# Attention and a Mish MLP on one core: the MLP in two phases through DRAM, with seven block products for w_out

## The chip, the cores and the metric

One core of one Trainium2 chip runs the whole program. The metric is device time in microseconds for one execution, from the first to the last instruction of the core. The engines are TensorE (PE, its weight loads PEld), VectorE (DVE), ScalarE (ACT), GpSimd (POOL) and SyncE (SP), which issues nearly all DMAs.

## The reference

Attention with a learned relative bias feeds a two-layer MLP with a Mish gate. All in float32; batch 4, 8 heads, 576 positions, 64 per head, so 2304 tokens of 512, and a hidden width of 2048.

```python
scores = scale * np.matmul(q, k.transpose(0, 1, 3, 2)) + bias        # bias: a small MLP of the relative position
attn = np.exp(scores - scores.max(-1, keepdims=True)); attn /= attn.sum(-1, keepdims=True) + 1e-09
x = np.matmul(attn, v).transpose(0, 2, 1, 3).reshape(2304, 512)
h = x @ w_in                                                          # 2304 x 2048
sp = np.where(h > 20.0, h, np.log1p(np.exp(np.minimum(h, 20.0))))
out = (h * np.tanh(sp)) @ w_out                                       # 2304 x 512
```

## The kernel before

The order of the work is written out by hand; each engine executes its instructions in program order and waits on semaphores.

**Bias stage** (to about 68 us). The relative bias of every head is computed and written to DRAM.

**Attention.** 16 pairs of heads and batches, each with five row groups c, make 80 steps; `step(n)` issues scores (PE, L220), the bias addition with the row maximum (DVE, L237), the exponentials (ACT, L252), the transposes of the step two before (PE, L287 and L290, evacuated by ACT, L295 and L296) and products with v (PE, L313, evacuated by DVE, L320). Two PSUM tiles hold the scores of one step. At the end of a step `split(n)` issues nine or ten pieces per five steps of the weights' conversion: w_in and w_out arrive as 64-bit floats and become 32-bit ones in four operations for a block of 128 x 512 (L118, or L116 on ACT; L121, L123, L125). All 32 blocks are converted here.

**MLP.** Every matmul is done three times with operands split in a high and a low part (`hi`, `lo`, float32r): hi x hi, hi x lo, lo x hi. Tokens go in blocks of 512, 512, 256, 512, 512. `hidden` (L589) makes 128 rows of h transposed for one block, 12 matmuls; `gate` computes the Mish as h * (e*e + 2e) / (e*e + 2e + 2) with e = exp(h), by ACT (Exp, Ln, Exp, a copy for ghi) and DVE (L595, L596, L606, L607, L612); `project` (L627) adds the product with 128 rows of w_out to the y tiles of the block in PSUM, three units behind `hidden`. The next block's x is loaded two units ahead of its splitting (`split_x`).

Of the kernel before, what the change touches and what calls it, by code (L numbers as in the profile page):

```python
# [16 lines left out]
HP = H // 2  # L17
# [9 lines left out]
E20 = 485165195.40979  # L27
# [4 lines left out]
NFC = DFF // P  # L32

# [11 lines left out]
def kernel(ctx: ExitStack, tc, qk, v, wb, w2, w_in, w_out, psia, psi4, rinv, eye, out):  # L45
# [21 lines left out]
    xa = sbuf("xa", side="right")  # L67
    dram = ctx.enter_context(tc.tile_pool(name="dram", bufs=1, space=DRAM))


    two = const.tile([P, 96], F32, name="two")
# [9 lines left out]
    order = [(kind, g, k) for g in range(4) for kind in "io" for k in range(4)]  # L81
    order.sort(key=lambda job: 4 * job[1] + (3.5 + job[2] if job[0] == "o" else 0))


    EARLY, MID = 4, 15
    MIDDLE = EARLY + MID
    ring = sbuf("ring").ring((len(order) - EARLY) * 2048 + 2560)
    w_hi, w_lo = {}, {}
    todo, w64, w32 = list(order), [], []

    def alloc_weights(jobs, p):
        for job in jobs:
            w_hi[job] = p.tile([P, 512], F32R, name="wh{}{}{}".format(*job))
            w_lo[job] = p.tile([P, 512], F32R, name="wl{}{}{}".format(*job))
# [12 lines left out]
    def conv_weights(on_act):  # L107

        job, w = w64.pop(0)
        late = order.index(job) >= EARLY
        c = (ring if late else convp).tile([P, 512], F32, name="w32")
        cu = c.bitcast(U32)
        if on_act:
            act.mul(c, w.bitcast(F32)[:, :, 1], 2.0 ** -112)  # L116
        else:
            dve.tensor_scalar(c, w.bitcast(F32)[:, :, 1], 2.0 ** -112, None, op0=ALU.mult)  # L118

        def parts():  # L120
            dve.tensor_scalar(w[:, :, 0], w[:, :, 0], 29, None, op0=ALU.logical_shift_right)  # L121
            yield False
            dve.scalar_tensor_tensor(cu, cu, 3, w[:, :, 0], op0=ALU.logical_shift_left, op1=ALU.bitwise_or)  # L123
            yield False
            dve.scalar_tensor_tensor(cu, w[:, :, 1], 0x80000000, cu, op0=ALU.bitwise_and, op1=ALU.bitwise_or)  # L125
            w32.append((job, c))
            yield True
        return parts()

    def split_weights(eng):  # L130
        job, c = w32.pop(0)
        if job not in w_hi:
            w_hi[job] = ring.tile([P, 512], F32R, name="wh{}{}{}".format(*job))
            w_lo[job] = ring.tile([P, 512], F32R, name="wl{}{}{}".format(*job))
        act.copy(w_hi[job], c)
        eng.tensor_tensor(w_lo[job], c, w_hi[job].bitcast(F32), op=ALU.subtract)
# [48 lines left out]
    def load_bias(hp, c):  # L185
# [3 lines left out]
        if c < 3 and hp % 2 == 0:  # L189
            pool_, name = ((xa, "xhi"), (xa, "xlo"), (x0, "xraw"))[c]  # L190
            t = pool_.tile([P, HP * TB], F32, name=name)[:, :2 * S]
        else:
            t = biasp.tile([P, 2 * S if c < 4 else S], F32, name=f"bias{c}")
# [135 lines left out]
    alloc_weights(order[:EARLY], wpool)  # L329

    x_raw, x_hi, x_lo = {}, {}, {}
    blocks = [(0, 512), (512, 512), (1024, 256), (1280, 512), (1792, 512)]

    def load_x(blk, p):
        t0, n = blocks[blk]
        raw = p.tile([P, HP, TB], F32, name="xraw", bufs=1)
# [19 lines left out]
    def ahead(n):  # L356
# [7 lines left out]
        if n == NS - 11:  # L364
            load_x(0, x0)
        if n == NS - 10:
            x_hi[0] = xa.tile([P, HP, TB], F32R, name="xhi")
            x_lo[0] = xa.tile([P, HP, TB], F32R, name="xlo")
# [8 lines left out]
    def split(n):  # L377

        i, x = divmod(n, 5)
        for _ in range(((2, 1, 2, 2, 2) if n > 25 else (2, 1, 3, 2, 2) if n > 4 else (0,) * 5)[x]):  # L380
            if not conv and w64:
                conv.append(conv_weights(x == 2))
            elif conv and next(conv[0]):
                conv.clear()
                load_weights()
                if w32[0][0] in order[:EARLY]:
                    split_weights(pool)
# [69 lines left out]
    dve.memset(two, 2.0)  # L457
# [99 lines left out]
    xp = sbuf("xp", 1, side="right")  # L557
    mp = sbuf("mp", 2, side="right")
    h_ps = psum("h_ps", 4, side="right")

    XPARTS = [(x, d) for x in "hl" for d in range(HP)]

    def split_x(blk, parts):
        n = blocks[blk][1]
        if blk not in x_hi:
            x_hi[blk] = (xp if blk % 2 else xa).tile([P, HP, TB], F32R, name="xhi")
# [8 lines left out]

    units = [(blk, tuple(range(f, f + TB // n))) for blk, (_, n) in enumerate(blocks) for f in range(0, NFC, TB // n)]
    h_t, gs, ys = {}, {}, {}

    LAG2 = 3

    def hidden(blk, fs):
        n = blocks[blk][1]
        h = h_ps.tile([P, TB], F32, name="h")
        for u, f in enumerate(fs):
            g4, r = divmod(f, 4)
            k = 0
            for w, x in ((w_hi, x_hi[blk]), (w_lo, x_hi[blk]), (w_hi, x_lo[blk])):
                for d in range(HP):
                    pe.matmul(h[:, u * n:(u + 1) * n], w["i", g4, d][:, r * P:(r + 1) * P], x[:, d, :n],  # L589
                              start=(k == 0), stop=(k == 11))  # L590
# [6 lines left out]
        h_t[blk, fs] = (h, e)  # L597

# [143 lines left out]
```

## Time and profile before

| | |
|---|---|
| median of 3 runs | 701.15 us (699.9, 701.15, 702.38) |
| span of the profiled execution | 700.9 us |
| PE, DVE, ACT, POOL busy | 672.9, 517.3, 458.4, 72.4 us |
| DMA | 81.88 MB, mean 117 GB/s |

Busy times are unions over the span. A PE instruction's end is modelled, so the time of a matmul in a stream is read from the distance of two starts. "Idle before" is what an engine waited ahead of an instruction, with the releaser behind the arrow.

### The profile page before, as it was taken

Reading aid. Unit: us, or ns where it says so; the run is one execution under the profiler, and the core shown is the slowest. Engines: PE = TensorE matmul, PEld = TensorE weight load, DVE = VectorE, ACT = ScalarE, POOL = GpSimd, SP = SyncE. Lnnn points to the kernel's source line nnn. Section 1 sums busy time; section 2 is a strip of 40 time slices with the busy share of each in tenths; the row PEclk is TensorE's granted clock in tenths of the full one; section 3 lists DMA queues with packets and bytes.
Section 4 is the critical chain, followed back from the end, with each engine's and each line's share of the span. In section 5 each row is a group of like instructions: output and inputs, shape, how many; then the busy total and the mean of one; then the engine's idle time right before and its main releaser. Section 6 shows DMA issues by size and latency. Waiting matters only on the chain.

```text
span 700.9 us, 13630 instructions
## 1 busy us (share of the span) xinstructions
PE 672.9 (96%) x5156; PEld 511.2 (73%) x5156; DVE 517.3 (74%) x1082; ACT 458.4 (65%) x987; POOL 72.4 (10%) x85
## 2 busy tenths in 40 slices
PE   5878999999999999999999999999999999999997
PEld 2224666776777666668888888889988888888886
DVE  7995898888988878868788566655775567665554
ACT  6895988888899888876675544444554455454443
POOL 0000142322222222710000000000000000000000
PEclk9999999999999999999999999999999999999999
DMA  4997688787778767204000120023005000010001
GB/s 150 318 285 228 195 273 263 216 284 225 245 234 266 241 231 240 55 22 116 1 1 0 66 56 1 1 76 106 1 1 150 1 1 0 1 60 1 1 0 60
DMA packets 46081, 81.88 MB, mean 117 GB/s; under 512 B 14400, under 2 KB 23104, under 8 KB 46016
## 3 DMA queue, kind: packets, MB, share of 16 engines
q1 hardware_dynamic: 43568, 72.70, 32.8%
q0 software_dynamic: 1872, 8.09, 3.9%
q8 instruction: 40, 0.66, 0.4%
q10 hardware_dynamic: 576, 0.22, 0.1%
q14 instruction: 25, 0.20, 0.1%
HBM read 60.60 MB, written 20.40 MB: 116 GB/s over the span
## 4 chain that ended last, share of the span: by engine, by line
PE 71%; ACT 9%; DVE 7%; DMA 3%; issue 2%; DVEq 0%; ACTq 0%
PE h L589 28%; PE y L627 28%; PE o L313 5%; PE s L220 5%; ACT pt L252 5%; DVE pt L237 4%; ACT main L295 3%; PE tp L287 3%; PE tp L290 1%; DMA w<-in_w_in_dram 1%; DMA w<-in_w_out_dram 1%; PE o L317 1%; DVE w L123 1%; DVE x L320 1%; DVE w L125 1%
## 5 line engine op out<-in xcount | busy, mean ns | idle before, releaser
L252 ACT ACTIVATE pt<-pt,m 128x576 f32<-128x576 f32 x144 | 112.2, 780 | 33.5 <-DVE m L237 32.9
L627 PE MATMUL y<-who,ghi 128*128 128x512 f32 x288 | 112.1, 389 | 0.0
L627 PE MATMUL y<-wlo,ghi 128*128 128x512 f32 x288 | 112.1, 389 | 0.0
L627 PE MATMUL y<-who,glo 128*128 128x512 f32 x288 | 112.0, 389 | 0.0
L611 ACT CAST ghi<-e 128x512 fp32r<-128x512 f32 x72 | 44.7, 621 | 93.5 <-DVE e L607 93.5
L237 DVE CUSTOM_DVE_ANT_0 pt<-s,bias 128x576 f32<-128x576 f32 (+1 forms) x112 | 81.3, 753 | 17.8 <-PE s L220 16.6
L594 ACT ACTIVATE e<-h 128x512 f32<-128x512 f32 x72 | 43.0, 597 | 65.9 <-PE h L589 65.7
L595 DVE TENSOR_SCALAR e<-e 128x512 f32<-128x512 f32 x72 | 30.6, 426 | 74.0 <-ACT e L594 74.0
L612 DVE TENSOR_TENSOR glo<-e,ghi 128x512 fp32r<-128x512 f32 x72 | 49.8, 692 | 44.9 <-ACT ghi L611 44.9
L589 PE MATMUL h<-xhi,whi 128*128 128x512 f32 (+1 forms) x320 | 79.1, 369 | 0.0
L589 PE MATMUL h<-xhi,wli 128*128 128x512 f32 (+1 forms) x320 | 78.7, 368 | 0.0
L589 PE MATMUL h<-xlo,whi 128*128 128x512 f32 (+1 forms) x320 | 78.7, 368 | 0.0
L313 PE MATMUL o<-main,vt 128*64 128x320 f32 (+1 forms) x512 | 73.8, 411 | 3.1 <-DVE x L320 3.0
L295 ACT COPY main<-tp 128x512 f32<-128x512 f32 x126 | 66.5, 577 | 2.0 <-DMA bias_d<-bt 1.9
L287 PE MATMUL tp<-ident,pt 64*128 64x64 f32 x1184 | 61.7, 227 | 6.3 <-ACT main L295 4.7
L589 PEld LDWEIGHTS h<-xhi,whi 128*128 128x128 f32 x320 | 57.1, 188 | 11.7 <-issue 0.7
L287 PEld LDWEIGHTS tp<-ident,pt 64*128 64x128 f32 x1184 | 53.5, 139 | 15.2 <-ACT main L295 13.1
L589 PEld LDWEIGHTS h<-xhi,wli 128*128 128x128 f32 x320 | 56.9, 189 | 10.0
L589 PEld LDWEIGHTS h<-xlo,whi 128*128 128x128 f32 x320 | 56.9, 189 | 10.0
L627 PEld LDWEIGHTS y<-who,glo 128*128 128x128 f32 x288 | 54.1, 188 | 11.3
L627 PEld LDWEIGHTS y<-who,ghi 128*128 128x128 f32 x288 | 54.1, 188 | 11.0
L627 PEld LDWEIGHTS y<-wlo,ghi 128*128 128x128 f32 x288 | 54.1, 188 | 10.9
(69 smaller groups left out, 1126.9 us busy)
## 6 DMA issues: line engine op xcount, KB each, us to landing
bias_d<-bt SPq DMA_DIRECT2D x36, 295.5 KB
w<-in_w_in_dram SPq DMA_DIRECT2D x16, 512.0 KB
w<-in_w_out_dram SPq DMA_DIRECT2D x16, 512.0 KB
qkhi<-in_qk_dram POOLq DMA_DIRECT2D x13, 608.0 KB, 4.5
rawqk<-in_qk_dram SPq DMA_DIRECT2D x13, 608.0 KB
vt<-in_v_dram SPq DMA_DIRECT2D x16, 320.0 KB
out_dram<-w SPq DMA_DIRECT2D x17, 256.0 KB
x_d<-x SPq DMA_DIRECT2D x32, 128.0 KB
```

What stands on the lines that cost most here:

```text
L220: pe.matmul(s[:, j, :SH], q[rows, c * P:(c + 1) * P], k[rows, KO + j * SH:KO + (j + 1) * SH], start=(t == 0), stop=(t == len(terms) - 1))
L237: dve.tensor_tensor_reduce(out=halves(pt[rows, sl]), in0=s[rows, :, :SH], in1=halves(bt[rows, sl]), scale=-0.125, scalar=BIG, op0=ALU.add, ...
L252: act.activation(ps, ps, AF.Exp, bias=m[:, u:u + 1], scale=-1.0, accum_out=sums[i][:, k:k + 1])
L287: pe.transpose(tp[:, k * 64:k * 64 + 64], pt[rows, c0:c0 + P], ident[rows, rows])
L295: copy(main[:, :, :, q0:q0 + 64], tp.rearrange("p (h k q) -> p h k q", h=2, k=4))
L313: pe.matmul(o[h * 64:h * 64 + 64, :w], vt[:, h, k, :], main[:, h, k, :], start=(k == 0), stop=False, **kw)
L589: pe.matmul(h[:, u * n:(u + 1) * n], w["i", g4, d][:, r * P:(r + 1) * P], x[:, d, :n], start=(k == 0), stop=(k == 11))
L594: act.activation(e, h, AF.Exp)
L595: dve.tensor_scalar(e, e, E20, None, op0=ALU.min)
L611: act.copy(ghi, e)
L612: dve.tensor_tensor(glo, e, ghi.bitcast(F32), op=ALU.subtract)
L627: pe.matmul(ys[blk][t], g[:, c0:c0 + P], w, start=(f == 0 and k == 0), stop=(f == NFC - 1 and k == 2))
```

## The change

The MLP falls into two phases. In the first, only `hidden` and the gate run, for all blocks: ACT computes the Mish in one activation (`AF.Mish`) from PSUM, and the activations g go to DRAM (`g_d`). For each block the tokens are cut in two halves and the hidden width in two halves, which gives four quarters A11, A12, A21, A22; what is stored is A11, S1 = A21 + A22 (added by POOL), A12 and A22. In the second phase, for each of nine tiles (128 tokens of each half), `prepare` forms the seven left operands of Strassen's scheme in Winograd's form and splits them in hi and lo, `multiply` does the seven products with combinations of w_out's quarters (`wc`, made by `combine` during the last block), and `leave` adds them up. A product accumulates hi x (hi and lo of w, side by side, 512 columns) and lo x hi (256 columns); the two halves are added at the end (`fold`). `split` issues one conversion piece per step and stops after the 16 blocks of w_in; w_out's blocks are converted during blocks 1 to 3 of the first phase. The order of the hidden rows within a block changes (`FORDER`), buffers are laid out anew.

```diff
-    order = [(kind, g, k) for g in range(4) for kind in "io" for k in range(4)]
...
+    order = [("i", g, k) for g in (0, 2, 1, 3) for k in range(HP)] + [("o", g, k) for g in range(4) for k in range(4)]
...
-        for _ in range(((2, 1, 2, 2, 2) if n > 25 else (2, 1, 3, 2, 2) if n > 4 else (0,) * 5)[x]):
...
+        for _ in range((1 if n > 4 else 0)):
+            convert(x == 2, order[EARLY + 11])
...
-        e = mp.tile([P, TB], F32, name="e", bufs=3)
-        act.activation(e, h, AF.Exp)
-        dve.tensor_scalar(e, e, E20, None, op0=ALU.min)
-        dve.scalar_tensor_tensor(e, e, 2.0, e, op0=ALU.add, op1=ALU.mult)
...
-        act.activation(r, e, AF.Ln, bias=two[:, 0:1])
-        act.activation(r, r, AF.Exp, scale=-1.0)
-        dve.tensor_tensor(e, h, e, op=ALU.mult)
-        dve.tensor_tensor(e, e, r, op=ALU.mult)
...
-        act.copy(ghi, e)
-        dve.tensor_tensor(glo, e, ghi.bitcast(F32), op=ALU.subtract)
...
-                for k, (g, w) in enumerate(((ghi, whi), (ghi, wlo), (glo, whi))):
-                    pe.matmul(ys[blk][t], g[:, c0:c0 + P], w,
-                              start=(f == 0 and k == 0), stop=(f == NFC - 1 and k == 2))
...
+        act.activation(g[:, c0:c0 + len(fs) * n], h_t.pop((blk, fs)), AF.Mish)
+        if fs[-1] >= 8:
+            del g_t[blk, j]
+            g = g.rearrange("p (k t) -> p k t", k=4)
+            pool.tensor_tensor(g[:, 1], g[:, 1], g[:, 3], op=ALU.add)
+            sp.dma_start(out=g_d[blk][:, :, j].rearrange("k p t -> p k t"), in_=g)
...
+    def combine(m):
+        if m in w_sum:
+            dve.tensor_tensor(w_src[m], *w_sum[m], op=ALU.subtract)
+        for half in (slice(0, 4), slice(4, 8)):
+            hi, lo = wc[m][:, half, 0:256], wc[m][:, half, 256:512]
+            act.copy(hi, w_src[m][:, half])
+            dve.tensor_tensor(lo, w_src[m][:, half], hi.bitcast(F32), op=ALU.subtract)
+        if m == 2:
+            dve.tensor_tensor(b11, b21, b11, op=ALU.subtract)
...
+        for k, r in enumerate(raws[p]):
+            sp.dma_start(out=r, in_=g_d[blk][k, :, :, u * P:(u + 1) * P])
...
+    def prepare(p, m):
+        a11, s1, a12, a22 = raws[p]
+        if m == 2:
+            dve.tensor_tensor(a11, s1, a11, op=ALU.subtract)
+        src = (a11, s1, a11, a12, s1, a11, a22)[m]
+        hi, lo = (slots[(7 * p + m) % 4][:, t] for t in range(2))
+        act.copy(hi, src)
+        dve.tensor_tensor(lo, src, hi.bitcast(F32), op=ALU.subtract)
+        if m == 3:
+            pool.tensor_tensor(s1, a22, a11, op=ALU.subtract)
+            pool.tensor_tensor(a11, a12, a11, op=ALU.subtract)
...
+        for f in range(8):
+            pe.matmul(o, hi[:, f], wc[m][:, f], start=(f == 0 and m in (0, 1, 3)), stop=False, **kw)
+            pe.matmul(o[:, 0:256], lo[:, f], wc[m][:, f, 0:256], start=False, stop=(f == 7), **kw)
...
+        if m == 0:
+            act.copy(p1s, a)
+        elif m == 1:
+            act.copy(p5s, c)
+        elif m == 2:
+            act.copy(u2s, a)
+        elif m == 3:
+            dve.tensor_tensor(ct[:, 0], p1s, b, op=ALU.add)
+        elif m == 4:
+            dve.tensor_tensor(ct[:, 3], p5s, a, op=ALU.add)
+        elif m == 5:
+            dve.tensor_tensor(ct[:, 1], u2s, c, op=ALU.add)
+            fold(0, 2)
...
+        elif m == 6:
+            last = p == len(tiles) - 1
+            if last:
+                fold(3, 4)
+            act.copy(ct[:, 2], a)
+            fold(2, 3 if last else 4)
...
+        if 1 <= blk <= 3:
+            for _ in range(2):
+                convert(True, None)
...
+    seq = [(p, m) for p in range(len(tiles)) for m in range(7)]
+    LEAD = 3
+    for n, (p, m) in enumerate(seq):
+        if n + LEAD < len(seq):
+            prepare(*seq[n + LEAD])
...
+        multiply(p, m)
+        leave(p, m)
```

The change moves instructions on DVE and PE. In attention, DVE's queue has this before, between the bias additions of a step with c = 2 and the next (w_ names are blocks of weights under conversion, x the product with v):

```order
L237 ISA pt,m<-s,xraw 128x576
L237 ISA m 128x1
L125 SCALAR_TENSOR_TENSOR w_3876<-w_3704,w_3876 128x512
L118 TENSOR_SCALAR w_3988<-w_3826 128x512
L320 COPY x<-o 128x320
L237 ISA pt,m<-s,bias_2897 128x576
```

After, the same place holds one piece of conversion:

```order
L243 ISA pt,m<-s,xraw 128x576
L243 ISA m 128x1
L128 TENSOR_SCALAR w_3563<-w_3563 128x512
L326 COPY x<-o 128x320
L243 ISA pt,m<-s,bias_2833 128x576
```

One of two pieces has left the step; the copy of x and the next addition follow one operation earlier. On PE, a unit of `hidden` and the products of an earlier unit alternate before (who and wlo are the parts of one block of w_out):

```order
L589 MATMUL h<-xlo,whi_129 128x512
L627 MATMUL y_5387<-who_5332,ghi 128x512
L627 MATMUL y_5387<-wlo_5333,ghi 128x512
L627 MATMUL y_5387<-who_5332,glo 128x512
L627 MATMUL y_5388<-who_5332,ghi 128x512
```

After, all units of `hidden` stand ahead of the first product (rows of the last block, then of the first tile; combo holds w_out's combination, gslot the split left operand):

```order
L603 MATMUL h<-xa,wearly 128x512 x48
L603 MATMUL h<-xa,lb 128x512 x48
L603 MATMUL h<-xa,lc 128x512 x96
L719 MATMUL y<-combo_5200,gslot_6306 128x512
L720 MATMUL y<-combo_5200,gslot_6306 128x256
```

The products have left the units, and come as pairs of a long and a short matmul. In the second phase DVE's queue holds, for one tile, the splits of the left operands (L702), one sum (L698), the additions to partial results (L739, L741, L743) and the folds (L730); nothing of the kind stood there before:

```order
L702 TENSOR_TENSOR gslot_6309<-quarters,gslot_6309 128x1024
L739 TENSOR_TENSOR quarters<-la,h 128x512
L702 TENSOR_TENSOR gslot_6306<-w_7533,gslot_6306 128x1024
L741 TENSOR_TENSOR quarters<-p5s,h 128x512
L702 TENSOR_TENSOR gslot_5201<-w_7534,gslot_5201 128x1024
L743 TENSOR_TENSOR quarters<-ld,y 128x512
L730 TENSOR_TENSOR quarters<-quarters 128x512
L698 TENSOR_TENSOR w_7533<-w_7534,w_7533 128x1024
L702 TENSOR_TENSOR gslot_6308<-w_7533,gslot_6308 128x1024
```

Each product has one split, prepared three products ahead.

## Rows read from the trace of the kernel before

**Rows 1.** The page: clock granted in 40 slices, and the chain by engine.

```profile
PEclk9999999999999999999999999999999999999999
...
PE 71%; ACT 9%; DVE 7%; DMA 3%; issue 2%; DVEq 0%; ACTq 0%
```

**Rows 2.** Windows: stretch, length, busy us of each engine, clock, DMA share, GB/s.

```profile
core 0: us, PE busy (x) PEld busy (x) DVE busy (x) ACT busy (x) POOL busy (x), PEclk, DMA share, GB/s
...
67.92:296.84 228.92, 221.96 (x2790) 157.79 (x2786) 198.53 (x497) 197.83 (x515) 67.76 (x77) 1.00 0.72 228
296.84:697.12 400.28, 400.28 (x1898) 332.80 (x1896) 263.29 (x434) 208.74 (x354) 4.23 (x3) 1.00 0.10 30
```

**Rows 3.** Timeline of PE and PEld in the MLP: start, duration, engine, instruction.

```profile
479.87 0.19 PEld L627 LDWEIGHTS y<-who,glo 128*128 128x128 f32 x1
...
481.00 0.64 PE L589 MATMUL h<-xhi,whi 128*128 128x256 f32 x4
...
483.87 0.40 PE L627 MATMUL y<-who,ghi 128*128 128x512 f32 x1
...
639.84 1.07 PE L589 MATMUL h<-xhi,whi 128*128 128x512 f32 x4
...
642.56 0.39 PE L627 MATMUL y<-who,ghi 128*128 128x512 f32 x1
...
645.28 1.07 PE L589 MATMUL h<-xhi,whi 128*128 128x512 f32 x4
```

**Rows 4.** Groups by line, attention: the weights' conversion on DVE and ACT.

```profile
L125 DVE SCALAR_TENSOR_TENSOR w<-w,w 128x512 uint32<-128x512 uint32 x32 | 24.1, 752 | 0.7
L123 DVE SCALAR_TENSOR_TENSOR w<-w,w 128x512 uint32<-128x512 uint32 x32 | 23.2, 726 | 0.7
...
L121 DVE TENSOR_SCALAR w<-w 128x512 uint32<-128x512 uint32 x32 | 15.8, 493 | 1.9 <-DMA w<-in_w_out_dram 1.8
L118 DVE TENSOR_SCALAR w<-w 128x512 f32<-128x512 f32 x24 | 11.5, 478 | 2.4 <-DMA w<-in_w_out_dram 1.7 <-DMA w<-in_w_in_dram 0.7
...
L116 ACT ACTIVATE w<-w 128x512 f32<-128x512 f32 x8 | 5.6, 706 | 0.0
```

**Rows 5.** Waits from 67.92 to 296.84: total us, times, longest.

```profile
ACT pt L252 <- DVE m L237: 30.6, 48, 2.2
DVE pt L237 <- PE s L220: 22.9, 32, 1.9
...
DVE w L121 <- DMA w<-in_w_out_dram: 1.8, 1, 1.8
DVE w L118 <- DMA w<-in_w_out_dram: 1.7, 2, 1.4
```

**Rows 6.** Timeline of DVE: first bias addition of four groups of five steps.

```profile
67.92 0.76 DVE L237 CUSTOM_DVE_ANT_0 pt<-s,xhi 128x576 f32<-128x576 f32 x1 [0.73 <-PE s L220]
...
130.63 0.75 DVE L237 CUSTOM_DVE_ANT_0 pt<-s,bias 128x576 f32<-128x576 f32 x1
...
145.30 0.76 DVE L237 CUSTOM_DVE_ANT_0 pt<-s,bias 128x576 f32<-128x576 f32 x1
...
282.86 0.76 DVE L237 CUSTOM_DVE_ANT_0 pt<-s,bias 128x576 f32<-128x576 f32 x1 [1.41 <-PE s L220]
```

**Rows 7.** Groups: DVE subtraction alone, DVE and POOL side by side (283 to 298 us).

```profile
L612 DVE TENSOR_TENSOR glo<-e,ghi 128x512 fp32r<-128x512 f32 x72 | 49.8, 692 | 44.9 <-ACT ghi L611 44.9
...
L373 DVE TENSOR_TENSOR xhi<-xraw,xlo 128x512 fp32r<-128x512 f32 x4 | 5.5, 1374 | 0.0
...
L374 POOL TENSOR_TENSOR xraw<-xraw,xlo 128x512 f32<-128x512 f32 x4 | 5.1, 1279 | 4.6 <-DVE xhi L373 4.6
```

**Rows 8.** Groups of ACT in the MLP.

```profile
L604 ACT ACTIVATE r<-e,two 128x512 f32<-128x512 f32 x72 | 51.5, 715 | 0.0
...
L611 ACT CAST ghi<-e 128x512 fp32r<-128x512 f32 x72 | 44.7, 621 | 93.5 <-DVE e L607 93.5
L594 ACT ACTIVATE e<-h 128x512 f32<-128x512 f32 x72 | 43.0, 597 | 65.9 <-PE h L589 65.7
...
L645 ACT COPY w<-y 128x512 f32<-128x512 f32 x8 | 4.7, 589 | 9.5 <-PE y L627 9.5
```

**Rows 9.** Timeline of the end.

```profile
696.73 0.39 PE L627 MATMUL y<-who,glo 128*128 128x512 f32 x1
697.16 0.42 DVE L638 COPY w<-y 128x256 f32<-128x256 f32 x1
...
698.02 0.36 ACTq L642 DMA_DIRECT2D out_dram<-r  x1
```

More of the change, by code (lines that the diff above doesn't have):

```diff
@@ L364, in ahead @@
         if n == NS - 11:
[L365 removed]
+            load_x(0, x0.tile([P, HP, TB], F32, name="xraw"))
         if n == NS - 10:
[L367 to L368 removed]
+            x_hi[0], x_lo[0] = (xa_t[:, t].bitcast(F32R) for t in range(2))
             load_r(0, x_lo[0].bitcast(F32), 0, HP)
@@ L573, in split_x, with w_at, hidden @@
                 dve.tensor_tensor(lo, raw, hi.bitcast(F32), op=ALU.subtract)
[L576 to L581, printed above, removed]
+    FORDER = [0, 1, 2, 3, 8, 9, 10, 11, 4, 12, 5, 13, 6, 14, 7, 15]
+    units = [(blk, i, (f,) if n == TB else (f, f + 8))
+             for blk, (_, n) in enumerate(blocks) for i, f in enumerate(FORDER if n == TB else range(8))]
+    h_t, g_t, n_g = {}, {}, [0]
+    def w_at(f, d):
+        return [x[:, f % 4] for x in w_split["i", f // 4, d]]
+    def hidden(blk, i, fs):
         n = blocks[blk][1]
@@ L663 @@
     wq = sbuf("wq")
[L664 to L687 removed]
+    y_ps = psum("y_ps", 4)
@@ new lines, with load_g @@
+    tiles = [(blk, u) for blk, (_, n) in enumerate(blocks) for u in range(n // 256)]
+    raws = {}
+    def load_g(p):
+        blk, u = tiles[p]
+        if p % 2 == 0:
+            w = [convp.tile([P, 512, 2], U32, name="w64").bitcast(F32).rearrange("p f t -> p (f t)") for _ in range(2)]
+            raws[p] = [w[0], w[1], la[:, 0:1024], c_early[0].rearrange("p a b -> p (a b)")]
+        else:
+            raws[p] = [rg[:, k:k + 1024] for k in (2048, 3072, 4096, 5120)]
+        raws[p] = [r.rearrange("p (f t) -> p f t", f=8) for r in raws[p]]
+        for k, r in enumerate(raws[p]):
+            sp.dma_start(out=r, in_=g_d[blk][k, :, :, u * P:(u + 1) * P])
@@ new lines, in reuse_x @@
+    def reuse_x():
+        slots.insert(0, rt.tile([P, 2, 8, P], F32R, name="gslot0"))
+        wc[1] = rt.tile([P, 8, 512], F32R, name="combo1")
+        slots.extend(rt.tile([P, 2, 8, P], F32R, name=f"gslot{k}") for k in (2, 3))
+    for k in range(2, len(units)):
+        blk, i, fs = units[k]
+        if blk + 1 < len(blocks):
+            w = len(fs)
+            if i == (6 if w == 1 else 1):
+                begin_x(blk + 1)
+            i0 = 8 if w == 1 else 3
+            if i0 <= i < i0 + 8 // w:
+                split_x(blk + 1, XPARTS[(i - i0) * w:(i - i0 + 1) * w])
+        if k > 2:
+            hidden(blk, i, fs)
+        for _ in range(2):
+            if w32:
+                split_weights(dve)
+        if 1 <= blk <= 3:
+            for _ in range(2):
+                convert(True, None)
+        if blk == 4:
+            if i == 0:
+                combine(0)
+                reuse_x()
+            elif i == 2:
+                combine(1)
+            elif i == 5:
+                combine(2)
+            elif i == 8:
+                load_g(0)
+            elif i == 9:
+                combine(3)
+            elif i == 11:
+                prepare(0, 0)
+            elif i == 13:
+                combine(4)
+            elif i == 14:
+                prepare(0, 1)
+        gate(blk, i, fs)
```

228 lines of the change are left out of this document (121 added, 107 removed).

## The prediction

> **What bounds the kernel now.** I read the page first: one clock level all the way (2.4 GHz, PEclk 9 or more in every slice), and a chain that is PE for 71%, ACT for 9%, DVE for 7% [rows 1]. That is a mean over two different stages, so the windows come next [rows 2]. From 296.84 us on (the MLP) PE is busy for all of 400.28 us; DVE has 263, ACT 209, the DMA engines a tenth. What is worth something there is PE time alone. From 67.92 to 296.84 us (attention) PE shows 222 of 229 us, but DVE and ACT have 198 each, and three engines so full that wait on each other in turn are one loop: ACT waits 30.6 us for the maxima of DVE's bias addition, DVE 22.9 us for PE's scores [rows 5]. Taking work from DVE can pay there too.
>
> What a matmul costs is read from starts, since the ends are modelled. Twelve matmuls of `hidden` with 512 columns start at 639.84, the next row follows at 642.56: 226.7 ns each. Twelve of `project` fill 642.56 to 645.28: the same. In the 256-token block 24 matmuls of 256 columns, each with its own weights, fill 481.00 to 483.87: 119.6 ns each [rows 3].
>
> **The change, part by part.**
>
> *The product.* Before: 18 row tiles x 16 f x 3 = 864 matmuls of 512 columns, 195.9 us. After: 9 tiles (of 128 rows from each half of a 256-token pair) x 7 products x 8 f = 504 pairs, each one 512-column matmul (hi against w's hi and lo side by side) and one of 256 (lo against hi), as the order rows of PE show. A pair is 226.7 + 119.6 = 346.3 ns, the sum 174.5 us: **-21.3 us**. By these two rows a matmul costs 12.5 ns (2 x 119.6 - 226.7) and each column 0.418 ns: an eighth fewer columns save 23.1 us, and 144 matmuls more take back 1.8. `hidden` keeps its matmuls. The alternation of 512 and 256 columns is not in the trace; from below its price is that of the two rows, from above a 256 costs as much as a 512 (rival 3). I take the rows, since the 256-column row also changes weights at every matmul.
>
> *Attention.* The 16 blocks of w_out are no longer converted there. A block is four operations, 0.48 + 0.49 + 0.73 + 0.75 us by the means; 120 of them on DVE are 74.6 us, and 8 on ACT 5.6 us [rows 4]. DVE keeps 61 of the 120 and ACT 3 of 8, so some 37 us leave DVE and 3.5 leave ACT. How much of that reaches the end? Bounds: nothing from below (all of it might stand in DVE's pauses). From above, ACT's whole wait of 30.6 us. Two readings lie between. First, ACT's wait less DVE's own wait for PE, which fewer conversions can't shorten: 30.6 - 22.9 = 7.7 us, and to it DVE's waits for w_out's DMAs, 1.8 + 1.7 = 3.5 us [rows 5]: 11 us. Second, a group of five steps (one head pair of one batch) takes (282.86 - 67.92) / 14 = 15.35 us on average, while the best one, from 130.63 to 145.30, takes 14.67 [rows 6]; were all 15 like it, 10 us would go. I take **-10 us** and keep 0 and -16 for the range. The second reading is not a floor, as that group carries conversions too.
>
> *The Mish.* Per 512 columns three passes of ACT and five of DVE become one ACT pass, a Mish out of PSUM that the trace doesn't hold. Nearest rows: 0.597 us for the Exp out of PSUM, 0.715 us for Ln [rows 8]. Even three times that stays under a unit's 2.72 us (twelve matmuls), and four PSUM banks cover the lateness of one: **0**. It needs another function table, loaded once ahead of the first Mish; no row has its price. What hides it is that the first result is needed four units later, and that ACT waits 65.9 us for PE over the MLP [rows 8].
>
> The Trainium skill (ScalarE: Activation LUTs, What ACT_TABLE_LOAD costs) gives about 2.66 us for a switch of tables and the same time per element for every function; by it the sum would grow by 2.7 us if the switch lay on PE's path. No row shows such a switch.
>
> *Through DRAM.* Every second unit POOL adds 256 columns and SP stores 512 KB; together 18.9 MB out in the 197 us of `hidden` (768 x 226.7 + 192 x 119.6 ns), then back in at 2.1 MB a tile, with 0.5 MB of results, in 19.4 us: some 135 GB/s against 228 GB/s that attention sustains [rows 2]. **0**; each load has eight products (22 us) between its buffers' release and its first reader. On SP's queue the stores wait for POOL ahead of the next block's x loads, which now have two units of 2.72 us, not two of 5.44. Late, they hold ACT's xhi copies and the Mish behind them in the queue; PSUM's four banks cover three units, 8 us. The conversion of w_out moves under blocks 1 to 3, 48 DVE pieces or 32 us in 110, where PE doesn't ask for DVE.
>
> *Second phase, ACT, DVE, POOL.* A tile has 7 x 346.3 x 8 = 19.4 us of PE. By the rows for 512 elements, doubled for 1,024 (an estimate that counts the fixed part twice): ACT 7 x 1.24 + 4 x 0.6 = 11.1 us [rows 8]; DVE 8 x 1.38 + 5 x 0.69 = 14.5 us [rows 7]; POOL 4 x 1.28 = 5.1 us. But a DVE operation beside POOL's took 1.374 us, not 0.692 [rows 7]; in POOL's 5.1 us DVE does half the work, so 14.5 + 2.5 = 17.0 us. Under 19.4, with operands prepared three products ahead: **0**, though DVE is the closest.
>
> *Joints.* When `hidden` ends, two products are prepared; the third takes a Mish, a copy and a subtraction (0.6 + 1.24 + 1.38 us) within the 5.5 us of these two: +0.5 us, between 0 and 3. At the end the last matmul starts at 696.73, and two half copies (0.42 us) on two engines and two DMAs of 128 KB follow, the second issued at 698.02 [rows 9]. After, one copy of 0.59, then one addition of 0.42, then 256 KB in one DMA: +0.5 us.
>
> *Sum.* Against the execution's own span, 700.9 us: -21.3 - 10 + 0.5 + 0.5 = -30.3, **671 us**. The runs' median is 701.15 (699.9 to 702.38), 0.04% off, so no correction; 0.3% is about what can be told from no change.
>
> **Rivals.**
> 1. *Attention gives nothing:* PE and ACT take up the slack, as each group's ACT work (198 us over all) and PE's waits suggest. For it: PE shows 97% there [rows 2]. Against it: the spread of the groups and the waits for w_out. 700.9 - 21.3 + 1 = 681 us (676 to 684).
> 2. *DVE becomes the bound of the second phase.* From 19.4 us per tile on, each further us costs 9 us. Against it: 17.0. If POOL slowed all of DVE's work, 14.5 x 1.99 = 28.8 us, 85 us more than PE: 756 us; up to 22.7 us per tile the kernel is still no slower. Mild form, 1 or 2 us a tile: 680 to 689 us. The Trainium skill (GPSIMD Engine Reference, Specifications) states that GpSimd shares its SBUF interface with VectorE when an instruction there has two SBUF inputs; all the splits here are such. The doubled duration in the row agrees.
> 3. *The change doesn't do what it says, and is slower:* weights that change ahead of a 512 can't be loaded behind a 256, so the short matmul costs as long as a long one. 504 x 2 x 226.7 = 228.5 us, +32.6: 700.9 + 32.6 - 10 + 1 = 725 us. It decides from 180 ns per short matmul on, attention's gain counted. For it: a weight load's own duration of 0.19 us [rows 3] is longer than the 0.107 of 256 columns (x 0.418 ns). Against it: 119.6 ns in a row where each short matmul has a load ahead of it.
> 4. *The first tile or the x loads make PE wait*, 3 to 8 us: 674 to 679 us, inside the forecast's range.
>
> **How the numbers follow.** Forecast with attention's gain between 5 and 16 us and joints up to 3 us: 664 to 678 us, 0.63 (rival 4 is in it for the most part). Rival 1: 0.18. Rival 2 in its mild form: 0.11, at its worst 0.02. Rival 3: 0.03. Something else, about no change: 0.03. The range runs from -16 us of attention without joint costs (663.6) to no gain there with 5 us at joints or in DVE (685.6): 663 to 686. Cases that end faster sum to 0.92, slower 0.05, no change 0.03.
>
> **What would show it.** The product's stretch: 504 pairs in 174 to 176 us, PE without a wait. If a 256-column matmul starts a 512 more than 125 ns later, rival 3 has begun. In PE's waits, a DVE split of a slot (line 702) as releaser means rival 2. Attention's fourteen groups: 205 us instead of 214.9, no DVE wait for w_out, ACT's wait for the maxima down by ten; if that wait stays and PE's own grow, rival 1. The forecast is wrong if a load of g from DRAM ends late, or if Mish is longer than 2 us.

## The result and the profile after

The changed kernel takes 680.59 us (median of 684.94, 679.86, 677.66 and 681.31) against 701.76 for the kernel before (701.15, 699.9, 702.38 and 704.88): ratio 0.97, 95% interval 0.9669 to 0.9731. It is faster by 21 us, inside the range of 663 to 686, but 9.6 us short of the forecast of 671. The profiled execution is the slowest of the four, with a span of 683.1 us, 17.8 under the 700.9 of before. One profile among the experiments (the extra matmul in each tile) was taken in a disturbed execution, with a granted clock of 0.75; its trace is read for nothing.

The page of the changed kernel: granted clock in 40 slices.

```profile
PEclk9999999999999999999999999999999999999999
```

Windows of the changed kernel: attention, the first phase of the MLP (`hidden`, Mish, stores of g), the second (the products). They answer to [rows 2].

```profile
core 0: us, PE busy (x) PEld busy (x) DVE busy (x) ACT busy (x) POOL busy (x), PEclk, DMA share, GB/s
67.17:294.27 227.10, 221.69 (x2792) 158.25 (x2788) 164.32 (x438) 194.32 (x510) 64.12 (x77) 0.99 0.62 197
294.27:498.43 204.16, 204.16 (x1034) 170.76 (x1033) 83.00 (x115) 81.72 (x142) 34.66 (x41) 1.00 0.56 175
498.43:678.70 180.27, 178.94 (x1009) 154.37 (x1007) 146.86 (x118) 84.91 (x101) 47.42 (x19) 1.00 0.39 121
```

The account of the 17.8 us: the start gives 0.75; attention 228.92 - 227.10 = 1.8, where 10 were forecast; the MLP from its first matmul to the start of its last one went from 399.9 us (296.84 to 696.73) to 384.2 (294.27 to 678.47), 15.7 where 20.8 were forecast; the tail takes back 0.5. So two terms came out small, by 8.2 and by 5.1 us.

*Attention.* DVE's bias additions that begin a group of five steps (the second, the seventh, the eighth and the last; the second stands at 67.17 as in [rows 6]), from the timeline of the changed kernel:

```profile
67.17 0.76 DVE L243 CUSTOM_DVE_ANT_0 pt<-s,xa 128x576 f32<-128x576 f32 x1 [0.72 <-PE s L226]
...
142.79 0.76 DVE L243 CUSTOM_DVE_ANT_0 pt<-s,bias 128x576 f32<-128x576 f32 x1 [0.80 <-PE s L226]
...
157.64 0.76 DVE L243 CUSTOM_DVE_ANT_0 pt<-s,bias 128x576 f32<-128x576 f32 x1 [0.79 <-PE s L226]
...
279.42 0.76 DVE L243 CUSTOM_DVE_ANT_0 pt<-s,bias 128x576 f32<-128x576 f32 x1 [3.76 <-PE s L226]
```

A settled group takes 14.85 us (142.79 to 157.64). Fourteen take 212.25, which is 15.16 on average: eleven lie between 14.74 and 15.09, two early ones take 15.61 and 15.48, and the last of the fourteen 17.46, with DVE 3.76 us without work at its end. The waits of the same stretch answer to [rows 5]:

```profile
DVE pt L243 <- PE s L226: 57.6, 63, 3.8
ACT pt L258 <- DVE m L243: 31.6, 46, 2.3
```

ACT's wait for the maxima has not moved (30.6 before). DVE's wait for scores went from 22.9 to 57.6: 34.7 us more, about the 34.2 us of work that left DVE in this stretch (198.5 to 164.3; 37 were forecast). The waits for w_out are gone.

*The last group.* Timelines of SP, POOL and PE of the changed kernel, one after the other:

```profile
258.90 1.36 SPq L330 DMA_DIRECT2D x_d<-x  x1
260.31 0.42 SPq L331 DMA_DIRECT2D x_d<-x  x1
265.76 0.57 SPq L341 DMA_DIRECT2D xraw<-x_d  x1
266.43 1.57 SPq L270 DMA_DIRECT2D r_d<-rt  x4
268.09 0.36 SPq L173 DMA_DIRECT2D rawqk<-in_qk_dram  x1
...
276.04 3.19 POOL L177 TENSOR_TENSOR qklo<-rawqk,qkhi 128x304 fp32r<-128x304 f32 x4 [15.65 <-DMA rawqk<-in_qk_dram]
...
275.39 0.73 PE L226 MATMUL s<-qkhi 64*128 64x288 f32 x2
277.70 0.40 PE L226 MATMUL s<-qklo,qkhi 64*128 64x288 f32 x2 [1.58 <-POOL qklo L177]
278.49 0.40 PE L226 MATMUL s<-qkhi,qklo 64*128 64x288 f32 x2 [0.39 <-POOL qklo L177]
```

Read backwards: PE waits for POOL's split of the last q and k; POOL waited 15.65 us for their load; SP issued it at 268.09, because after 260.31 it stood at the first load of x. For what, the chain of waits of the changed kernel tells:

```profile
258.90 6.79 DMA x_d<-x
...
265.76 5.18 DMA xraw<-x_d
```

A write of x to DRAM, issued at 258.90, took 6.79 us, and the load of x that reads it was behind it, with q and k in the queue behind that. In the kernel before, the same split ran from 279.28 to 282.77, beside the scores that needed it (from 281.17 on), and no wait of PE for it is recorded: it came barely in time. After the change, attention reaches its last group but one 5.5 us earlier (261.97 against 267.45), while the load of q and k is issued only 2.85 us earlier (268.09 against 270.94).

*The products.* PE in the middle of the second phase, timeline of the changed kernel; starts answer to [rows 3]:

```profile
599.79 0.40 PE L719 MATMUL h<-combo,gslot 128*128 128x512 f32 x1
600.03 0.28 PE L720 MATMUL h<-combo,gslot 128*128 128x256 f32 x1
600.14 0.40 PE L719 MATMUL h<-combo,gslot 128*128 128x512 f32 x1
...
601.91 0.40 PE L719 MATMUL h<-combo,gslot 128*128 128x512 f32 x1
```

Six pairs from 599.79 to 601.91 are 353.3 ns each, 7 more than forecast: a 512 after a 256 starts 113 to 120 ns later, a 256 after a 512 starts 233 to 241 later. Eight tiles take 19.78 us, the first 21.86. All waits of PE in the second phase:

```profile
PE y L719 <- DVE quarters L741: 0.7, 1, 0.7
PE h L720 <- DVE gslot L702: 0.3, 1, 0.3
PE y L720 <- DVE gslot L702: 0.3, 1, 0.3
```

All three lie in the first tile (517.39, 513.83, 510.43); by the starts they cost 0.9, 0.5 and 0.5 us, and the matmul after each comes another 0.1 late. Behind them is DVE beside POOL. The groups of the splits, duration as least, median and most ns, and then timeline rows of DVE and of POOL:

```profile
L702 DVE TENSOR_TENSOR gslot<-w,gslot x30: 1210/1226/3356, 486.6 to 669.0; 128x1024 fp32r<-128x1024 f32 x30
...
L702 DVE TENSOR_TENSOR gslot<-la,gslot x5: 1210/3414/3422, 503.5 to 662.9; 128x1024 fp32r<-128x1024 f32 x5
```

```profile
500.26 3.36 DVE L702 TENSOR_TENSOR gslot<-w,gslot 128x1024 fp32r<-128x1024 f32 x1 [3.00 <-ACT gslot L701]
503.54 1.21 DVE L702 TENSOR_TENSOR gslot<-la,gslot 128x1024 fp32r<-128x1024 f32 x1
504.67 4.56 DVE L674 TENSOR_TENSOR lc<-quarters,lc 128x1024 fp32r<-128x1024 f32 x2
...
500.12 2.41 POOL L704 TENSOR_TENSOR w<-w,w 128x1024 f32<-128x1024 f32 x1
503.75 3.27 POOL L705 TENSOR_TENSOR w<-la,w 128x1024 f32<-128x1024 f32 x1 [1.22 <-issue]
```

A split of 1,024 elements per partition takes 1.21 us alone and 3.36 to 3.42 beside one of POOL's. The first tile has four such splits more, for the last two combinations of w_out (L674), and one of those met POOL too.

*The Mish.* From the timeline of ACT: one load of a function table, then activations of 0.60 us (L615, mean 598 ns).

```profile
299.23 1.28 ACT L615 ACT_TABLE_LOAD   x1
300.52 0.60 ACT L615 ACTIVATE g<-h 128x512 f32<-128x512 f32 x1
```

### The profile page after: what moved, and what is told of

Its sections match the earlier page's. It is cut to its first block, busy times and chain, and to the rows that moved or that the text cites. A ratio compares the mean times of both kernels' runs of the same rounds, so it can differ in the third digit from the quotient of the medians.

```text
span 683.1 us, 13785 instructions
## 1 busy us (share of the span) xinstructions
PE 655.8 (96%) x5300; PEld 504.1 (74%) x5300; DVE 449.6 (66%) x821; ACT 413.2 (60%) x871; POOL 146.6 (21%) x142
## 4 chain that ended last, share of the span: by engine, by line
PE 72%; ACT 15%; DMA 5%; issue 4%; DVE 4%; POOL 0%; SPq 0%; DVEq 0%; ACTq 0%
PE h L603 29%; PE y L719 8%; PE h L719 8%; ACT pt L258 6%; PE o L319 5%; PE s L226 5%; PE y L720 4%; PE h L720 4%; ACT main L301 4%; PE bps L534 3%; PE tp L293 3%; PE tp L296 2%; DVE pt L243 1%; PE o L323 1%; ACT bt L516 1%
## 5 line engine op out<-in xcount | busy, mean ns | idle before, releaser
L615 ACT ACTIVATE g<-h 128x512 f32<-128x512 f32 x72 | 42.7, 598 | 77.3 <-PE h L603 65.0
L177 POOL TENSOR_TENSOR qklo<-rawqk,qkhi 128x304 fp32r<-128x304 f32 x52 | 42.1, 834 | 124.7 <-DMA rawqk<-in_qk_dram 117.3
L603 PE MATMUL h<-xa,lc 128*128 128x512 f32 (+1 forms) x288 | 55.5, 354 | 0.0
L702 DVE TENSOR_TENSOR gslot<-w,gslot 128x1024 fp32r<-128x1024 f32 x30 | 43.3, 1455 | 15.4 <-ACT gslot L701 15.4
L603 PEld LDWEIGHTS h<-xa,lc 128*128 128x128 f32 x288 | 47.6, 189 | 7.5
L702 DVE TENSOR_TENSOR gslot<-quarters,gslot 128x1024 fp32r<-128x1024 f32 x28 | 47.0, 1705 | 7.9 <-ACT gslot L701 7.9
L226 PE MATMUL s<-qkhi 64*128 64x288 f32 x260 | 51.3, 346 | 0.3 <-DVE m L243 0.3
L226 PEld LDWEIGHTS s<-qkhi 64*128 64x128 f32 x260 | 28.6, 185 | 30.6 <-DVE m L243 16.3
L226 PE MATMUL s<-qklo,qkhi 64*128 64x288 f32 x260 | 42.9, 299 | 1.6 <-POOL qklo L177 1.6
L504 DVE TENSOR_SCALAR ht<-at,bb 128x576 f32<-128x576 f32 (+17 forms) x123 | 44.1, 432 | 0.0
L226 PE MATMUL s<-qkhi,qklo 64*128 64x288 f32 x260 | 41.3, 292 | 0.4 <-POOL qklo L177 0.4
```

What stands on the lines that cost most here:

```text
L226: pe.matmul(s[:, j, :SH], q[rows, c * P:(c + 1) * P], k[rows, KO + j * SH:KO + (j + 1) * SH], start=(t == 0), stop=(t == len(terms) - 1))
L603: pe.matmul(h[:, u * n:(u + 1) * n], w_at(f, d)[t], x[:, d, :n], start=(k == 0), stop=(k == 11))
L702: dve.tensor_tensor(lo, src, hi.bitcast(F32), op=ALU.subtract)
```

## The experiments

Three questions: what VectorE's relief is worth in attention, what the stall at the last q and k is worth, and where the second phase's 5 us are. Edits are against the changed kernel. The kernel before was timed beside them three times, with medians of 702.55, 702.54 and 702.32 us. A kernel's own runs differ by 2 to 9 us.

**VectorE's load put back.**

```diff
+            for _ in range(4 if n >= EARLY and job[0] == "i" else 0):
+                dve.scalar_tensor_tensor(cu, hi, 0x80000000, cu, op0=ALU.bitwise_and, op1=ALU.bitwise_or)
+                yield False
             dve.scalar_tensor_tensor(cu, hi, 0x80000000, cu, op0=ALU.bitwise_and, op1=ALU.bitwise_or)
...
-        for _ in range((1 if n > 4 else 0)):
+        for _ in range((2 if n > 4 else 0)):
```

> The changed kernel with VectorE's load in attention put back to about that of before: the last conversion instruction of each of the twelve blocks of w_in that are converted there is issued five times (it gives the same value each time), two per step where there was one, so that attention holds about 110 conversion instructions on VectorE, not 61. Theory A (the steady group fell from a mean of 15.35 to 14.85 us because VectorE lost half of its conversions, and the floor at 14.85 is TensorE's and ScalarE's): the groups go back to a mean of 15.2 to 15.4 and the first hidden matmul starts 4 to 7 us later, near 299 to 301; whole time 0.6 to 1% over the changed kernel's. Rival B (VectorE's conversions lie in its idle time; the groups settled for another reason, such as the weights of w_out no longer being loaded then): groups within 0.15 us of 14.85, hidden start within 2 us of 294.3.

689.08 us (686.34 to 690.58), ratio to before 0.9794 (0.9751 to 0.9838). Its attention in the windows, and its waits there:

```profile
68.81:299.95 231.14, 224.75 (x2790) 158.28 (x2786) 201.79 (x485) 195.26 (x511) 70.38 (x77) 1.00 0.61 194
```

```profile
ACT pt L261 <- DVE m L246: 36.9, 48, 3.4
DVE pt L246 <- PE s L229: 23.9, 25, 2.4
```

VectorE is busy for 201.8 us again (198.5 before), its wait for scores is back at 23.9, fourteen groups take 217.2 us, 15.5 each, and the first hidden matmul starts at 299.95. Theory A holds, though only the first two of w_out's sixteen loads fall into attention here, as in the changed kernel: the relief, of a load slightly over that of before, is worth 7.3 us of attention's 14 groups against the 209.8 that they take without the stall (next run). The pieces of conversion were used up early in this run: eleven groups with nine or ten pieces on DVE take 15.3 to 16.1 us, the last two, with none, 14.84. In the next run groups with five pieces take 14.85 and the last, with none, 14.84: from five pieces down nothing more is gained.

**The last q and k ahead of x.**

```diff
-        if x == 0 and i + 1 < NPAIR:
+        if x == 0 and i + 1 < NPAIR and n != NS - 10:
             load_raw(i + 1)
+        if n == NS - 11:
+            load_raw(NPAIR - 1)
```

> The changed kernel with one edit: the load of the last head pair's q, k and v is issued in step 69, ahead of the load of the first x block, where it stood behind it on SP. Theory A (the last group of attention lost its time because SP stood 5.4 us at the load of x, until 265.76, with the load of q and k queued behind it, so that the split of q and k on GpSimd ended at 279.23 and TensorE stood from 275.5 to 278.5): step 74 falls from 5.20 to about 2.9 us and the first hidden matmul starts about 2.5 us earlier, near 291.8; whole time 0.3 to 0.4% under the changed kernel's, about 678 where that one gives 680.6. Rival B (the stall is only exchanged for another: the load of x now lands later and the first hidden product waits for its x): step 74 falls, but the first hidden matmul stays within 0.5 us of 294.27. Rival C (the late load is chance of one execution): no difference of the medians.

680.96 us (678.71 to 682.15), ratio 0.9685 (0.9649 to 0.9722). Windows, then rows of SP and POOL:

```profile
67.13:290.96 223.83, 220.19 (x2790) 157.02 (x2786) 165.92 (x438) 193.81 (x510) 64.31 (x77) 1.00 0.62 200
```

```profile
261.21 0.40 SPq L173 DMA_DIRECT2D rawqk<-in_qk_dram  x1
...
266.31 0.57 SPq L341 DMA_DIRECT2D xraw<-x_d  x1
...
267.76 3.21 POOL L177 TENSOR_TENSOR qklo<-rawqk,qkhi 128x304 fp32r<-128x304 f32 x4 [7.24 <-DMA rawqk<-in_qk_dram]
```

The load of x is as late as before, but q and k no longer stand behind it; step 74 takes 2.58 us, the fourteen groups 209.8 and the first hidden matmul starts at 290.96. The place is shown. What PE itself waited for in attention, in the kernel before and then in this run:

```profile
PE o L313 <- DVE x L320: 3.0, 5, 0.8
PE tp L287 <- ACT main L295: 2.3, 13, 0.2
```

```profile
PE tp L293 <- ACT main L301: 1.0, 5, 0.2
PE s L226 <- DVE m L243: 0.3, 1, 0.3
```

The products with v no longer wait for DVE's copy of an earlier x out of PSUM; with VectorE's load put back they do again (1.8 us, 6 times). A settled group has PE busy for 14.67 of its 14.85 us (142.98 to 157.83). The whole time is not shorter by what the ratios to before can tell (0.9685 here, 0.97 and, below, 0.9689 without the edit).

**The 512-column matmuls of a product together.**

```diff
             pe.matmul(o, hi[:, f], wc[m][:, f], start=(f == 0 and m in (0, 1, 3)), stop=False, **kw)
+        for f in range(8):
             pe.matmul(o[:, 0:256], lo[:, f], wc[m][:, f, 0:256], start=False, stop=(f == 7), **kw)
```

> The changed kernel with one edit: within a block product the eight 512-column matmuls come first and then the eight 256-column ones, where they alternated; same 504 pairs. Theory A (a 512-column matmul followed by a 256-column one holds the next start for 236 ns where one followed by another of 512 columns took 226.7, so the alternation costs about 6.5 ns per pair): the pair falls from 353 to about 347 ns and the product from 180.3 to about 177 us, 0.4 to 0.5% of the whole. Rival B (the 236 ns come from the traffic of the other engines or from the operands of this stage, not from the order): the median start to start of two matmuls of 512 columns is 236 ns here too and the product stays within 0.5 us of 180.3.

682.36 us (680.75 to 685.18), ratio 0.9705 (0.967 to 0.9741). Two 512s start 226 to 236 ns apart, with a median of 231, two 256s 120 ns, and a tile takes 19.55 us, 349 ns per pair: between the theories. PE in the first two products:

```profile
496.88 1.98 PE L719 MATMUL y<-combo,gslot 128*128 128x512 f32 x8
498.69 1.12 PE L721 MATMUL y<-combo,gslot 128*128 128x256 f32 x8
499.64 2.00 PE L719 MATMUL h<-combo,gslot 128*128 128x512 f32 x8
501.49 1.11 PE L721 MATMUL h<-combo,gslot 128*128 128x256 f32 x8
```

The first eight 512s follow the 512s of `hidden` and take 1.81 us from start to start, 226.7 ns each. The second eight follow 256s and take 1.85: five starts are 228 to 236 ns apart, the last three 226 or 227, and so it goes in nearly all later products. So what ran before sets a matmul's price here, as theory A has it; the stage is the same for both groups, so its operands and traffic (rival B) do not. The first tile takes 23.39, since PE now waits in one piece ahead of product 6, for DVE, and then runs for some time at the lower clock: nine starts are 426 or 213 ns apart. Wait, and windows of 15 us in which the clock shows:

```profile
PE y L719 <- DVE quarters L742: 2.1, 1, 2.1
```

```profile
505.00:520.00 15.00, 12.92 (x66) 11.01 (x65) 14.26 (x14) 5.40 (x7) 1.04 (x2) 0.89 0.72 217
```

A granted clock of 0.89 over the stretch is 2.4 GHz with 1.2 for a fifth of it. And the run before, with the order unchanged, had tiles of 19.41 us from the second on: pairs of 346.7 ns. So strict alternation does not have to cost 353 either.

**Three edits at once.** Both edits above, and the last two combinations of w_out later:

```diff
-        if n == 0:
+        if n == 1:
             combine(5)
-        elif n == 1:
+        elif n == 3:
             combine(6)
```

> The changed kernel with three edits: the last q and k loaded ahead of x, the 512-column matmuls of a product ahead of its 256-column ones, and the last two combinations of w_out's blocks made two and three products later, in the first tile (products 1 and 3, where they were 0 and 1). Theory A for each: -2.5 us, -3 us and -1 to -2 us (TensorE stood about 1.8 us in the first tile, at 510.4, 513.8 and 517.4, for splits that VectorE did behind those combinations), so 6 to 7 us or 0.9 to 1.0% under the changed kernel, about 674. If the rivals hold (the stall moves, the 236 ns stay, the first tile waits elsewhere) under 2 us.

680.89 us (678.68 to 681.65), ratio 0.9678 (0.9645 to 0.9712): the rivals' case. The stall is gone (step 74 at 2.58), but tiles take 19.55 us and PE's starts stand 2.35 us apart ahead of product 6, for DVE's addition of two partial results (the clock stayed at 1.00 here). Making the combinations later left that wait as long as in the grouped run (2.36 us).

**The changed kernel again.**

> The changed kernel as it is, timed beside the others on one chip. Theory A (the stall at the last q and k is in every execution, since SP's queue stands in the same order each time): step 74 of the attention takes 4.7 to 5.3 us again, and the median is 2 to 3.5 us over that of the kernel with q and k first. Theory B (the pair of matmuls of 512 and 256 columns settles at 347 or at 353 ns by chance of the execution, in one order as in the other): the pair is either of the two here, and its difference, 504 times 6 ns or 3 us, is of the size by which executions of one kernel differ. Rival (the pair depends on the kernel's text): 353 ns again.

682.17 us (678.17 to 683.47), ratio 0.9689 (0.9654 to 0.9724). Theory A falls: SP reached the load of x at 262.66 this time, step 74 took 2.91 us, and `hidden` began at 290.95, as with q and k first. The stall depends on when one write of x to DRAM lands: with SP's order unchanged, step 74 took 5.20, 4.78 (grouped), 5.16 (the next run), 2.91 and, in a slower attention with VectorE's load put back, 2.58 us; with q and k first 2.57 or 2.58 in all six profiles that are read. Pairs 353 ns again, which theory B and its rival both allow.

**POOL's differences on VectorE.**

```diff
-            pool.tensor_tensor(s1, a22, a11, op=ALU.subtract)
-            pool.tensor_tensor(a11, a12, a11, op=ALU.subtract)
+            dve.tensor_tensor(s1, a22, a11, op=ALU.subtract)
+            dve.tensor_tensor(a11, a12, a11, op=ALU.subtract)
```

> The changed kernel with one edit: the two differences of blocks of g that GpSimd makes for each tile of the product are made by VectorE, in the same place. Theory A (a subtraction of 128x1024 takes VectorE 1.21 us alone and 3.36 to 3.43 us while GpSimd makes one of its own beside it, so GpSimd's two cost VectorE 4.4 us per tile and would take it 2.4 us itself; in the first tile, where VectorE also makes the last combinations, TensorE stood 1.8 us for it): no split over 1.5 us is left, VectorE's busy time in the product falls from 147 to about 128 us, the first tile falls from 21.9 to about 20 us and the other eight stay; 1.5 to 2 us of the whole, 0.2 to 0.3%. Rival B (VectorE's own two subtractions come at the worst moment and TensorE waits for them): first tile 22 us or longer.

678.38 us (676.88 to 682.11), ratio 0.9649 (0.9616 to 0.9682). The same group as above, and the second phase in the windows:

```profile
L702 DVE TENSOR_TENSOR gslot<-w,gslot x30: 1217/1225/1305, 485.8 to 666.2; 128x1024 fp32r<-128x1024 f32 x30
```

```profile
497.57:675.90 178.33, 178.33 (x1009) 154.21 (x1007) 137.32 (x136) 84.11 (x101) 0.74 (x1) 1.00 0.40 123
```

No split is over 1.31 us, PE is busy from end to end, the first tile takes 19.89 us and the others 19.79. DVE does 18 operations more and is busy for 137.3 us, not 146.9: less relief than expected (128): POOL had cost DVE (146.9 + 18 x 1.22 - 137.3) / 9 = 3.5 us per tile, not 4.4. Theory A's 2 us on PE are there.

**Both: q and k first, differences on VectorE.**

> The changed kernel with two edits: the last q and k loaded ahead of x, and the two differences of each tile made by VectorE. Theory A: 3.3 us from the attention's end and 1.5 to 2 us from the first tile, so about 5 us or 0.7% under the changed kernel in the same call; the time is then near 675 to 676. Rival: one or both are covered by something else and the sum is under 2 us.

676.93 us (675.43 to 680.08), ratio 0.9631 (0.96 to 0.9663), 5.2 us under the changed kernel timed beside it: theory A's sum. The ranges of the runs overlap a little. Step 74 takes 2.58 us, the first tile 19.90. But the two profiled executions (680.08 and 681.68 us, both with pairs of 353) differ by 1.6 us only, because that execution of the changed kernel had no stall, so where all of the 5.2 us come from is not shown. The six times here lie in two heaps, 675.4 to 677.0 and 679.5 to 680.1; a rhythm of PE that changes from execution to execution (see the next run) would do that, but one execution of each kernel was profiled.

**And the combinations later.**

> The edits of the run before (q and k first, differences on VectorE), and the last two combinations of w_out's blocks made in products 1 and 3 of the first tile, where they were made in products 0 and 1. Theory A (what is left of the first tile's wait is VectorE's work in a heap at its start): first tile within 0.3 us of the others, at most 0.5 us under the run before. Rival B (the combinations then come late for products 5 and 6, as in the run that also grouped the matmuls, where TensorE stood 2.35 us): first tile 0.5 us or more over that of the run before.

680.13 us (675.72 to 681.06), ratio 0.9659 (0.9626 to 0.9691): no gain. The first tile takes 20.03 us, 0.13 over the run before (neither theory), most of it at 353 ns per pair and with two starts 0.34 us apart ahead of product 6. But the profiled execution, at 675.72 us, is the fastest of its six, and its pairs are short:

```profile
599.70 0.40 PE L721 MATMUL h<-wearly,gslot 128*128 128x512 f32 x1
...
601.78 0.40 PE L721 MATMUL h<-lb,gslot 128*128 128x512 f32 x1
```

Six pairs from 599.70 to 601.78, 346.7 ns each. In all eight profiles with strict alternation (the next run's included) the product begins with pairs of 353. By the end of the first tile three have passed to 347 and five stand at 353, one of these (VectorE's load put back) after most of a product at 347 between two waits. What stands then is kept for eight tiles: 448 x 6.6 ns = 3.0 us.

**An odd matmul at the start.**

```diff
+        if p == 0 and m == 0:
+            pe.matmul(o[:, 0:64], hi[:, 0], wc[m][:, 0, 0:64], start=True, stop=True, **kw)
```

> The kernel with q and k first and the differences on VectorE, and one matmul more: ahead of the first of the product's 504 pairs a matmul of 64 columns into the same bank, whose result the pair's own start writes over. In all profiles the product began with pairs of 353 ns; where TensorE waited in the first tile, it came back either at 353 or at 347 ns and kept that to the end. Theory A (the two rhythms are two ways in which starts of 512 and 256 columns can fall, and any change of the distance between two starts can pass from one to the other): the one extra matmul gives pairs of another length than 353 from the start, perhaps 347, which is 3 us of the whole. Rival B (only a real wait, in which TensorE's queue runs dry, changes the rhythm): 353 at the start as before, the time within 0.2 us of the kernel without it, save for what the wait at product 6 of the first tile (173 ns there) then decides.

677.95 us (677.23 to 678.91), ratio 0.9664 (0.964 to 0.9687). Between the theories: 353 ns from the second pair on in spite of the odd matmul, against A; but in product 6 of the first tile the rhythm passes to 347 where no wait of PE shows and one start is late by a few ns, against B.

**An odd matmul in each tile.** The same with `m == 0` and 128 columns.

> As the run before, but with an extra matmul of 128 columns ahead of each tile, nine in all, about 0.06 us each. Theory A: the rhythm can differ from tile to tile, and at least one tile is at 347 ns per pair while another is at 353. Rival B: nine tiles at 353 (or all alike after the first), and 0.5 us more than without.

679.10 us (678.43 to 680.12), ratio 0.9678 (0.9654 to 0.9702). Its trace is not read, so what the rhythm did can't be told.

**Every second pair turned.**

```diff
+            if f % 2:
+                pe.matmul(o[:, 0:256], lo[:, f], wc[m][:, f, 0:256], start=False, stop=False, **kw)
             pe.matmul(o, hi[:, f], wc[m][:, f], start=(f == 0 and m in (0, 1, 3)), stop=(f == 7), **kw)
-            pe.matmul(o[:, 0:256], lo[:, f], wc[m][:, f, 0:256], start=False, stop=(f == 7), **kw)
+            if not f % 2:
+                pe.matmul(o[:, 0:256], lo[:, f], wc[m][:, f, 0:256], start=False, stop=False, **kw)
```

> The kernel with q and k first and the differences on VectorE, with the order of every second pair turned: 512, 256, 256, 512, 512, 256, 256, 512 columns; same matmuls. Theory A (the 353 ns belong to the strict alternation of lengths; of two matmuls of one length after the other the hidden layer shows 226.7 and 119.6 ns in every profile): between 346 and 350 ns per pair on the mean, and the product 1.5 to 3.5 us shorter than at 353. Rival B (each change of length costs what it did, but there are half as many): about 350 ns, 1.7 us. Rival C (any mixture of lengths has the slow rhythm; grouped by eights the mean was 349.6): 349 to 353.

678.15 us (676.56 to 679.17), ratio 0.9661 (0.9635 to 0.9687). A tile takes 19.51 us, 348 ns per pair, from the first product on, and a delay of 0.4 us ahead of product 6 does not change it: inside A's bounds, though on the median it is no faster than strict alternation.

## Why the prediction was right, and where its terms were off

- **Direction and range: right.** The bound was read rightly: PE is busy for 204.16 of 204.16 us in the first phase and 178.9 of 180.3 in the second, and fewer columns on PE came out as time. That the range holds is in part luck: the forecast's own case (664 to 678) is missed, and 680.59 lies on the 681 of rival 1, by other terms than that rival's, as attention did gain and the product fell short.
- **The product, -21.3: mis-sized by 5.1 us.** The step "I take the rows, since the 256-column row also changes weights at every matmul" took two streams of one length each for a mixed one. Measured in the profiled execution: 504 x 7.0 ns = 3.5 us more, and 2.1 us in the first tile, against a joint that cost 0.5 less than forecast. 347 ns per pair, the forecast's figure, does occur (three profiles of eight), and then the product takes 175.0 to 177.0 us. What the rows could not show is the price of a change of length: in the grouped run the same 512 takes 226.7 ns behind others and up to 236 behind 256s. Rival 3 has nothing for it: no 512 starts more than 120 ns after a 256, the first tile's waits apart.
- **Attention, -10: mis-sized, and the largest miss.** Measured -1.8 in the profiled execution and -5.1 where the last q and k don't stall it. The failing step is the second reading, "were all 15 like it": the best group of before (14.67, behind one of 15.54) is under what the loop settles at, 14.85 with half the conversions gone and 14.84 with none. Two early groups keep 15.5 to 15.6, and PE's own work in attention, 220 of 224 us without the stall, leaves little more. The bound to read was PE's: 7.0 us idle before, 5.3 of them waits for DVE's copies of x and ACT's copies. The first reading failed in its other half: ACT's wait for maxima was to shrink and didn't; the relief went into DVE's wait for PE. Rival 1 named this mechanism, and the truth lies halfway to it: of its sign, ACT's wait stayed, but PE's idle time fell, from 7.0 to 3.6 us without the stall. The run with VectorE's load put back shows that the 5 us are VectorE's relief and not the absence of w_out's loads.
- **What wasn't foreseen: a late load on SP.** The text counted the queue of the first phase, not that of the last group, where the split of before was only just in time.
- **Mish, 0: right.** The activation takes 0.598 us as the Exp row said, and the table load of 1.28 us lies under a unit of `hidden`. That "no row has its price" was a misreading: the trace of before has such a load at its start, also of 1.28 us. The Trainium skill (ScalarE: Activation LUTs, What ACT_TABLE_LOAD costs) gives 2.66 us for a switch, made up of 1.28 for the load and 1.38 for a drain. The trace agrees on the load and shows no drain: ACT's last copy ends at 299.21, the load starts at 299.23, and the Mish starts as it ends. The rows decide.
- **Through DRAM, 0: right.** 175 GB/s in the first phase, 121 in the second, and no load of g among PE's waits.
- **Second phase, 0: right after the first tile, by another split of the work.** DVE alone is faster than estimated (1.21 us, not 1.38) and beside POOL slower (a factor of 2.8, not 2). From 520 us on it is busy for 82% of the time, 16.2 us per tile against 17.0 forecast. In the first tile rival 4 came true in small, 2.1 us, through rival 2's mechanism, and giving POOL's two differences to DVE removed it. The Trainium skill (GPSIMD Engine Reference, Specifications) names that mechanism, a shared SBUF interface that contends with VectorE instructions of two SBUF inputs; the 1.21 against 3.36 us agree.
- **Tail, +0.5: right** (4.63 us from the last matmul's start to the end, 4.17 before).

## What to carry to other kernels

Work taken off an engine in a loop of three pays until the next one is full: read what PE's own work leaves free there (229 - 222 us here) before the waits of the others, which only change names. An engine's slack on average does not cover its heap at a joint: list what it has to do in the first tile, and with whom it shares the memory there. And when a stage gets shorter, look at every load that stands behind a DRAM round trip in the same queue; a load that doesn't depend on it goes first.

## What the hardware showed that was not expected

- One and the same stream of alternating 512- and 256-column matmuls, at a granted clock of 1.00, has two steady rhythms, 353.3 and 346.7 ns per pair (starts 233, 236, 241 and 113, 117, 120 in turn, or 230 and 117). The shorter one also occurs with starts of 230 to 233 and 112 to 118. The rhythm changed in the first tile alone, at starts of PE there that were 0.34 to 1.24 us apart and once (the odd matmul) at one that was late by a few ns; then it is kept for eight tiles, 155 to 158 us, and is worth 3 us here. What chooses between them is open.
- A matmul's price in a mixed stream depends on what ran before it: in the grouped product eight 512s behind the 512s of `hidden` are 226.7 ns apart; behind 256s the first five are 228 to 236 apart and the last three 226 or 227, with the same shapes and a weight load each.
- DVE's subtraction of 128x1024 from SBUF takes 1.21 us and up to 3.42 us beside GpSimd's, which itself takes 2.4 to 3.3; both on DVE take 2.4 us. Here GpSimd's help cost more than it gave.
